# Moving the first state sums of units 0 and 1 behind one first-layer block in a fused RWKV-5 and SiLU kernel

## Chip, cores and metric

The kernel runs on one core of a Trainium2 chip. The metric is the device time of one execution in microseconds (us), given as the median over runs. The core has five engines with instruction queues of their own: TensorE (PE, with weight loads shown as PEld), VectorE (DVE), ScalarE (ACT), GpSimd (POOL) and SyncE (SP, which here only issues DMAs).

## What is computed

A recurrent attention (4 batches, 8 heads, 768 steps, head size 48), and behind it a two-layer network with SiLU on all 3072 tokens (width 384, hidden 2048):

```python
for t in range(S):
    kt, vt, rt = k[:, :, t], v[:, :, t], r[:, :, t]
    cur = einsum('bhd,bhe->bhde', u[None] * kt, vt)
    y[:, :, t] = einsum('bhd,bhde->bhe', rt, state + cur)
    state = w[None, :, :, None] * state + einsum('bhd,bhe->bhde', kt, vt)
...
x = y.transpose(0, 2, 1, 3).reshape(B * S, H * D)
h = x @ w_in
g = h * (1.0 / (1.0 + exp(-h)))
out = g @ w_out
```

## The kernel before

The sequence is cut into 6 chunks of 128 steps; a chunk of one batch is a **unit**, numbered chunk by chunk, so units 0 to 3 are the first chunk of the four batches, units 4 to 7 the second, and so on to 23. For a unit the kernel turns r and k on TensorE (step T), weights them with powers of the decay on VectorE (rT, kT), multiplies them to scores (P, or D for two units at once), masks these (n, m), and multiplies with v to get the outputs (V, Z). The term with u is formed on GpSimd (ku, ru, vu) with a sum on VectorE (rd). The state that a unit hands to the next chunk of its batch is a sum over its 128 steps of decayed k times v: kc is that decayed k (GpSimd, step kc), v16 the cast v (ScalarE, step v16). For units of the first chunk there is no state to add to, so the sums of a pair of batches come from one step, S (`first_sums`), into one PSUM buffer "sp". Two steps read it: st copies it to the running state `st` on VectorE, and scA (ScalarE) or sc (VectorE) copies it in f16 into the layout that the next chunk's outputs read.

The outputs of a chunk, turned (yT) and copied (xT on ScalarE, xTD on VectorE), feed the network. L*b.f* is a block of its first layer: the matmuls of hidden slices from f on for the batches that b names ("0" batches 0 and 1, "2" batches 2 and 3, both with two slices of 256 columns, so six matmuls; "4" all four batches, one slice of 512 columns, three matmuls). G*b.f* is its SiLU on ScalarE. The second layer follows later (line 628), spread as filler between the attention steps of later units.

All PSUM tiles of these steps except the turned inputs and the scores share one tag, "moe", with four buffers. A new tile takes the buffer that has been free longest, and its first write waits for the last reader of the tile before. The weights win (four pieces, i_q) and wout (four pieces, i_o) are loaded by GpSimd's queue, nearly all of r, k and v by SyncE's.

The order of instructions is the program's own (a manual schedule): no scheduler changes it. For the first eight units it is a string of steps, `order`, which a loop runs word by word; from unit 6 on a loop over pairs of units follows. Each engine runs its own instructions in the order of that string. The steps around the change are S0 (sums of units 0 and 1, line 419), L0.6 and G0.4 (lines 606 and 615), xT2 and xTD3 (line 595), kc1 and kc2 (line 248), st0 (line 441), scA0 (line 430), and further on Q4 (sums of units 4 and 5, line 478).

```python
def first_sums(i):
    sp = ps.tile([128, 512], FP, name="sp", tag="moe", bufs=4)
...
    for p in range(NP):
        for e in range(2):
            for j in range(2):
...
                    kc[(i + e) % NIN][:, h, :], L(i + e)["v16"][:, h, :],
```

So S0 goes through the four head pairs p, and in each takes unit 0 (two heads j), then unit 1.

Of the kernel before, what the change touches and what calls it, by code (L numbers as in the profile page):

```python
# [16 lines left out]
def kernel(  # L17
# [13 lines left out]
    B, H, S, D = r.shape  # L31
# [127 lines left out]
    lamC = cst.tile([128, H, D], FP)  # L159
    lamH = cst.tile([128, H, D], FP)  # L160
# [4 lines left out]
    lamN = cst.tile([128, H, D], FP)  # L165
# [522 lines left out]
    def piece(word, f):  # L688
# [30 lines left out]
        ur kz0 id itr lr0 wy pd0 ak0 cz2 kz3 itc wr mk wx cz1 mh lnw eK cg3 lamK kz4 kz1 lk1  # L719
        id16 lr1 pd3 lr3 lk3 clear 6*spin lv0 cg0 lv1 kz7 ak2 ar2 ku0 lv3 lv2 kz2 lr5 ub pd1 lv4  # L720
        lr4 lk4 lv5 pd2 lk5 lk7 lr6 lk6 uc T0 1*spin T1 lr7 lv7 kT0 pa4 rT0 ru0 ku1 v160 pd5 lv6
        rT1 kz6 rd0 kT1 wb ru1 P0 n0 2*spin rd1 P1 i_q0 vu0 lnwb T2 n1 v161 2*spin lamC lamH lamN pa6 pa7 V0 tab rT2 e0 kT2 ku2 T3 1*spin yT0 V1 kz5 i_q1 vu1 ru2 xT0 e1 P2 yT1 kT3 rT3
        rd2 ku3 xT1 v162 P3 ru3 n2 rd3 v163 n3 L0.0 vu2 kc0 1*spin G0.0 vu3 V2 L0.2 V3 G0.2 L0.4
        e2 i_q2 e3 kc1 yT2 yT3 S0 G0.4 xT2 xTD3 kc2 L0.6 L2.4 G0.6 st0 L2.0 scA0 v164 kc3 L2.6
        ku4 i_q3 v165 L2.2 T4 rT4 kT4 G2.4 ru4 G2.2 T5 G2.0 G2.6 L4.8 G4.8 L4.10 kT5 G4.10 L4.9
        kc4 ku5 S2 L4.11 rd4 rT5 st2 sc2 kc5 sd4 ru5 G4.9 G4.11 rA4 vu4 i_o0 Q4 D4 rA5 s1_4 ku7
        L4.12 rd5 vu5 m4 s2_4 G4.12 L4.13 G4.13 T6 Z4 L4.14 G4.14 L4.15 z4 yT4 2*spin yT5 i_o2
        i_o1 ku6 xT4 xT5 rT6 T7 G4.15 rT7 v167 sd6 kT6 v166 ru6 lr8 kc6 kc7 H H rd6 i_o3 H vu6
        lr9 rP7 rA6 sn4 H H lk8 lk9 sx4 lv9 lv8 ru7 kT7
    """  # L730
    for word in order.split():
        if "*" in word:
# [119 lines left out]
```

## Time and profile before

| | us |
|---|---|
| median of 3 runs | 184.46 |
| lowest and highest run | 183.74, 186.0 |
| profiled execution, its own time | 184.8 |
| span in its profile | 183.1 |

The span runs from the first to the last instruction of the profiled execution. Its granted TensorE clock is 1.0 throughout. Numbers with an L are lines of the kernel. In a timeline row stand the start, the length, the engine, line, operation, the tiles written and read, the shapes and the number of instructions merged; in brackets, the idle time of the engine before them and what ended it. In a row of a stretch stand its length, then for PE, PEld, DVE, ACT and POOL the busy time and the instructions, then the granted clock, the share of the 16 DMA engines and GB/s.

### The profile page before, as it was taken

Reading aid. Unit: us, or ns where it says so; the run is one execution under the profiler, and the core shown is the slowest. Engines: PE = TensorE matmul, PEld = TensorE weight load, DVE = VectorE, ACT = ScalarE, POOL = GpSimd, SP = SyncE. Lnnn points to the kernel's source line nnn. Section 1 sums busy time; section 2 is a strip of 40 time slices with the busy share of each in tenths; the row PEclk is TensorE's granted clock in tenths of the full one; section 3 lists DMA queues with packets and bytes.
Section 4 is the critical chain, followed back from the end, with each engine's and each line's share of the span. In section 5 each row is a group of like instructions: output and inputs, shape, how many; then the busy total and the mean of one; then the engine's idle time right before and its main releaser. Section 6 shows DMA issues by size and latency. Waiting matters only on the chain.

```text
span 183.1 us, 6612 instructions
## 1 busy us (share of the span) xinstructions
PE 175.7 (96%) x2801; PEld 114.1 (62%) x2801; DVE 116.1 (63%) x227; ACT 117.1 (64%) x212; POOL 129.3 (71%) x179
## 2 busy tenths in 40 slices
PE   7998899999999999999999899999999999999993
PEld 2566695588657976656547556647656566555562
DVE  4699729797798975955956945866944974000120
ACT  4468478599236796398687378787677781299100
POOL 7999999998899989959979769879769700000000
PEclk9999999999999999999999999999999999999999
DMA  5999999899588999999799999599699201410022
GB/s 90 238 218 196 196 195 196 138 216 222 99 174 211 159 213 197 178 188 206 130 183 150 181 194 185 127 183 184 156 200 245 48 4 47 129 43 0 12 77 86
DMA packets 102865, 27.89 MB, mean 152 GB/s; under 512 B 97586, under 2 KB 102324, under 8 KB 102836
## 3 DMA queue, kind: packets, MB, share of 16 engines
q1 hardware_dynamic: 97184, 23.67, 66.2%
q0 software_dynamic: 2176, 3.15, 10.1%
q10 hardware_dynamic: 3476, 0.66, 1.8%
q8 instruction: 22, 0.36, 0.8%
q14 instruction: 7, 0.06, 0.1%
HBM read 20.45 MB, written 4.72 MB: 137 GB/s over the span
## 4 chain that ended last, share of the span: by engine, by line
PE 76%; POOL 9%; DMA 5%; issue 3%; DVE 2%; ACT 2%; POOLq 0%; ACTq 0%; SPq 0%
PE ops L628 29%; PE hps L606 28%; PE att L455 5%; PE att L272 4%; DMA blocks<-planes 3%; POOL ku L240 2%; DMA kin<-in_k_dram 2%; PE sp L478 2%; PE zs L181 2%; POOL rku_f L245 2%; PE ops L653 1%; POOL vu L258 1%; PE yp L561 1%; PE yp L552 1%; ACT kT L326 1%
## 5 line engine op out<-in xcount | busy, mean ns | idle before, releaser
L606 PE MATMUL hps<-xT,win 128*128 128x512 f16 (+1 forms) x360 | 66.3, 338 | 0.0
L615 ACT ACTIVATE gT<-hps 128x512 f16<-128x512 f32 x96 | 55.3, 598 | 13.0 <-PE hps L606 9.8
L628 PE MATMUL ops<-wout,gT 128*128 128x384 f16 x368 | 63.0, 326 | 0.3
L606 PEld LDWEIGHTS <-win 128*128 128x128 f16 x360 | 38.8, 114 | 21.0 <-issue 0.2
L628 PEld LDWEIGHTS <-gT 128*128 128x128 f16 x368 | 35.0, 98 | 24.3 <-ACT gT L615 1.4
L401 DVE TENSOR_TENSOR y<-yp,vu 64x384 f16<-64x384 f32 (+1 forms) x34 | 18.9, 556 | 11.3 <-PE yp L561 6.1
L245 POOL TENSOR_TENSOR rku_f<-ku,u_bc 128x384 f32<-128x384 f32 x24 | 24.0, 1001 | 1.7 <-DVE u_bc L208 0.4
L240 POOL TENSOR_TENSOR ku<-kin,rin 128x384 f32<-128x384 f32 x24 | 24.5, 1020 | 0.0
L258 POOL TENSOR_TENSOR vu<-vin,rku 128x384 f32<-128x384 f32 x24 | 19.6, 829 | 6.4 <-DVE rku L253 6.3
L634 ACT COPY osb<-ops 128x384 f32<-128x384 f32 x20 | 9.4, 476 | 17.5 <-PE ops L628 11.8
L289 DVE TENSOR_TENSOR rT<-att,lamR 112x512 f16<-112x512 f32 (+1 forms) x26 | 17.8, 685 | 4.1 <-PE att L272 3.8
L326 ACT COPY kT<-blocks 112x1024 uint16<-112x1024 uint16 x14 | 15.6, 1161 | 7.3 <-DMA blocks<-planes 7.2
L495 DVE TENSOR_TENSOR s<-sp,sdec 112x384 f32<-112x384 f32 x10 | 5.6, 558 | 15.9 <-PE sp L478 15.3
L636 DVE COPY osb<-ops 128x384 f32<-128x384 f32 x3 | 1.7, 558 | 21.3 <-PE ops L628 21.3
L462 DVE TENSOR_TENSOR am<-att,maskH 128x1024 f16<-128x1024 f32 x10 | 12.2, 1224 | 3.7 <-PE att L455 3.7
L343 DVE TENSOR_TENSOR rX<-att,lamR 48x256 f16<-48x256 f32 x32 | 13.5, 422 | 0.5
L314 POOL TENSOR_TENSOR lnw_bc<-kin,lamN 128x384 f32<-128x384 f32 x7 | 7.0, 999 | 8.1 <-DMA kin<-in_k_dram 5.3
L253 DVE TENSOR_REDUCE rku<-rku_f 128x8 f32<-128x384 f32 x24 | 12.5, 545 | 0.3 <-POOL rku_f L245 0.3
L434 ACT CAST s1h<-s 48x384 f16<-48x384 f32 x16 | 8.2, 509 | 6.7 <-DVE s L495 6.6
L455 PE MATMUL att<-rT,kT 48*64 48x64 f32 x640 | 11.9, 220 | 0.5 <-issue 0.5
L455 PEld LDWEIGHTS att<-rT,kT 48*64 48x64 f32 x640 | 10.6, 135 | 0.6 <-issue 0.6
L263 ACT CAST v<-vin 128x384 f16<-128x384 f32 x16 | 7.8, 510 | 4.2 <-DMA vin<-in_v_dram 4.1
(106 smaller groups left out, 215.9 us busy)
## 6 DMA issues: line engine op xcount, KB each, us to landing
vin<-in_v_dram SPq DMA_DIRECT2D x24, 192.0 KB, 4.2
rin<-in_r_dram SPq DMA_DIRECT2D x23, 192.0 KB, 4.2
out_dram<-osb SPq DMA_DIRECT2D x23, 192.0 KB, 3.3
kin<-in_k_dram SPq DMA_DIRECT2D x22, 192.0 KB, 3.7
win<-in_moe_w_in_dram POOLq DMA_DIRECT2D x4, 384.0 KB, 6.8
wout<-in_moe_w_out_dram POOLq DMA_DIRECT2D x4, 384.0 KB, 6.6
kin<-in_k_dram ACTq DMA_DIRECT2D x2, 192.0 KB, 3.7
rin<-in_r_dram ACTq DMA_DIRECT2D x1, 192.0 KB
```

The lines of the kernel that those rows point to most:

```text
L240: eng.tensor_tensor(out=L(i)["ku"], in0=kin[i % NIN][:, :, 0:D], in1=rin[i % NIN][:, :, 0:D], op=ALU.mult)
L245: eng.tensor_tensor(out=L(i)["rku_f"], in0=L(i)["ku"], in1=u_bc, op=ALU.mult)
L253: nc.vector.tensor_reduce(out=L(i)["rku"], in_=L(i)["rku_f"], axis=mybir.AxisListType.X, op=ALU.add)
L258: eng.tensor_tensor(out=L(i)["vu"], in0=vin[i % NIN], in1=L(i)["rku"].unsqueeze(2).broadcast_to([128, H, D]), op=ALU.mult)
L289: nc.vector.tensor_tensor(out=L(i)[key].rearrange("p g (y t) -> p y g t", y=2), in0=L(i)["t"][0:PR, :, x], in1=lam, op=ALU.mult)
L326: nc.scalar.copy(out=L(i)["kT"].rearrange("p g t -> p (g t)").bitcast(U16) .rearrange("p (n y) -> p n y", y=2), in_=turned[0:PR, i % 2].re ...
L343: nc.vector.tensor_tensor(out=rx[here], in0=L(i)["t"][there, x, 0], in1=(lamM if by_planes(i) else lamR)[there, :, 0:HC], op=ALU.mult)
L401: nc.vector.tensor_tensor(out=y16[a], in0=y[b, 0:HD], in1=vu[a], op=ALU.add)
L455: nc.tensor.matmul(a[o0:o0 + HC, j, e, p, :], kT[r0:r0 + D, p, HC * x:HC * x + HC], rT[r0:r0 + D, p, HC * x:HC * x + HC], start=True, stop ...
L606: nc.tensor.matmul(hps[:, f, :].rearrange("p (b t) -> p b t", b=nb), win[(ft + f) // 4].rearrange("p q (t c) -> p q t c", c=4) [:, q, :, ( ...
L615: nc.scalar.activation(out=gts[sc][:, ft:ft + m, b0 * C:(b0 + nb) * C], in_=hpss[b0, ft], func=AF.Silu)
L628: nc.tensor.matmul(opss[b], gts[sc][:, ft, b * C:(b + 1) * C], wout[:, ft, :], start=(ft == 0), stop=(ft == NFT - 1))
```

## The change

S0 is moved in the string from behind yT3 to behind L0.6, ahead of L2.4. The lines below it are wrapped anew; no other word changes its place.

```diff
-        e2 i_q2 e3 kc1 yT2 yT3 S0 G0.4 xT2 xTD3 kc2 L0.6 L2.4 G0.6 st0 L2.0 scA0 v164 kc3 L2.6
+        L0.4 e2 i_q2 e3 kc1 yT2 yT3 G0.4 xT2 xTD3 kc2 L0.6 S0 L2.4 G0.6 st0 L2.0 scA0 v164 kc3
```

More of the change, by code (lines that the diff above doesn't have):

```diff
@@ L721 @@
         lr4 lk4 lv5 pd2 lk5 lk7 lr6 lk6 uc T0 1*spin T1 lr7 lv7 kT0 pa4 rT0 ru0 ku1 v160 pd5 lv6
-        rT1 kz6 rd0 kT1 wb ru1 P0 n0 2*spin rd1 P1 i_q0 vu0 lnwb T2 n1 v161 2*spin lamC lamH lamN pa6 pa7 V0 tab rT2 e0 kT2 ku2 T3 1*spin yT0 V1 kz5 i_q1 vu1 ru2 xT0 e1 P2 yT1 kT3 rT3
-        rd2 ku3 xT1 v162 P3 ru3 n2 rd3 v163 n3 L0.0 vu2 kc0 1*spin G0.0 vu3 V2 L0.2 V3 G0.2 L0.4
-        e2 i_q2 e3 kc1 yT2 yT3 S0 G0.4 xT2 xTD3 kc2 L0.6 L2.4 G0.6 st0 L2.0 scA0 v164 kc3 L2.6
[L725 to L729, printed above, removed]
+        rT1 kz6 rd0 kT1 wb ru1 P0 n0 2*spin rd1 P1 i_q0 vu0 lnwb T2 n1 v161 2*spin lamC lamH
+        lamN pa6 pa7 V0 tab rT2 e0 kT2 ku2 T3 1*spin yT0 V1 kz5 i_q1 vu1 ru2 xT0 e1 P2 yT1 kT3
+        rT3 rd2 ku3 xT1 v162 P3 ru3 n2 rd3 v163 n3 L0.0 vu2 kc0 1*spin G0.0 vu3 V2 L0.2 V3 G0.2
+        L0.4 e2 i_q2 e3 kc1 yT2 yT3 G0.4 xT2 xTD3 kc2 L0.6 S0 L2.4 G0.6 st0 L2.0 scA0 v164 kc3
+        L2.6 ku4 i_q3 v165 L2.2 T4 rT4 kT4 G2.4 ru4 G2.2 T5 G2.0 G2.6 L4.8 G4.8 L4.10 kT5 G4.10
+        L4.9 kc4 ku5 S2 L4.11 rd4 rT5 st2 sc2 kc5 sd4 ru5 G4.9 G4.11 rA4 vu4 i_o0 Q4 D4 rA5 s1_4
+        ku7 L4.12 rd5 vu5 m4 s2_4 G4.12 L4.13 G4.13 T6 Z4 L4.14 G4.14 L4.15 z4 yT4 2*spin yT5
+        i_o2 i_o1 ku6 xT4 xT5 rT6 T7 G4.15 rT7 v167 sd6 kT6 v166 ru6 lr8 kc6 kc7 H H rd6 i_o3 H
+        vu6 lr9 rP7 rA6 sn4 H H lk8 lk9 sx4 lv9 lv8 ru7 kT7
     """
```

## The prediction

> **What bounds the kernel now.** I read the page first (busy shares, slices), then the chain of waits in order of time, then the timeline around the moved step, then who waited for whom on TensorE. The page:
>
> ```profile
> PE 175.7 (96%) x2801; PEld 114.1 (62%) x2801; DVE 116.1 (63%) x227; ACT 117.1 (64%) x212; POOL 129.3 (71%) x179
> ...
> PE   7998899999999999999999899999999999999993
> ...
> POOL 7999999998899989959979769879769700000000
> ...
> DMA  5999999899588999999799999599699201410022
> ...
> DMA packets 102865, 27.89 MB, mean 152 GB/s; under 512 B 97586, under 2 KB 102324, under 8 KB 102836
> ```
>
> TensorE (PE) is the only engine that is full (9 is 90% or more) in every slice from the ninth to the last but one; GpSimd (POOL) and the DMA engines are full only in the first two thirds. A busy PE need not be a PE at its rate, so I look at how fast it goes, in the chain of waits in order of time (start, length, what), and at stretches of the span:
>
> ```profile
> 21.57 1.01 POOL kc L248
> ...
> 22.64 0.40 PE sp L419 x14
> 23.04 3.40 PE hps L606 x30
> ...
> 48.48 7.26 PE ops L628 x44
> ```
>
> ```profile
> 21.50:33.00 11.50, 10.55 (x212) 8.05 (x211) 6.58 (x14) 9.40 (x19) 11.46 (x14) 1.00 1.05 181
> 33.00:70.00 37.00, 37.00 (x711) 28.17 (x713) 30.59 (x59) 24.24 (x44) 34.42 (x44) 1.00 0.94 182
> ```
>
> 44 second-layer matmuls of 384 columns take 7.26 us, 165 ns each, or 2.3 columns a ns; 30 first-layer matmuls of 256 columns take 3.40 us, 113 ns each, the same rate. From 33 to 70 us PE is busy for all of 37.00 us at a granted clock of 1.00. What can still be won there is nothing; between 21.5 and 33 us PE is idle for 0.95 us (11.50 less 10.55), and there GpSimd is busy for 11.46 of 11.50 us. The moved step lies in that stretch.
>
> **The change.** S0 is 16 small matmuls with their weight loads (line 419, kc of units 0 and 1 against v16) into one PSUM buffer. It issues nothing on any other engine and no DMA. It moves behind G0.4, xT2 (ScalarE), xTD3 (VectorE), kc2 (GpSimd) and L0.6 (PE); as the engines have orders of their own, the only order that changes is PE's: S0 and the six matmuls of block L0.6 change places. PE before:
>
> ```profile
> 21.52 0.50 PE L591 MATMUL yT<-ident,y 128*128 128x128 f16 x6
> 21.94 0.21 PE L419 MATMUL sp<-v,kc 128*64 128x48 f16 x2
> 22.64 0.40 PE L419 MATMUL sp<-v,kc 128*64 128x48 f16 x14 [0.48 <-POOL kc L248]
> 22.97 3.47 PE L606 MATMUL hps<-xT,win 128*128 128x256 f16 x30
> 26.37 0.43 PE L272 MATMUL att<-ident,rin 64*112 64x64 f32 x8
> ...
> 27.41 2.13 PE L606 MATMUL hps<-xT,win 128*128 128x512 f16 x9
> ...
> 30.61 0.44 PE L478 MATMUL sp<-v,kc 64*64 64x48 f16 x32
> ...
> 32.48 0.33 PE L455 MATMUL att<-rT,kT 48*64 48x64 f32 x3 [0.47 <-issue]
> 32.75 1.49 PE L606 MATMUL hps<-xT,win 128*128 128x512 f16 x6
> ```
>
> The first two matmuls of S0 (unit 0) start at 21.94, the third (unit 1) waits for kc1, which GpSimd ends at 21.57 + 1.01 = 22.58, and starts at 22.64; the queue behind it holds L0.6 and all further PE work. This is the stall that goes. The other engines around it:
>
> ```profile
> 20.35 1.18 DVE L401 TENSOR_TENSOR y<-yp,vu 128x384 f16<-128x384 f32 x2
> ...
> 20.75 0.80 POOL L84 DMA_DIRECT2D win<-in_moe_w_in_dram x1
> ...
> 21.57 2.92 POOL L248 TENSOR_TENSOR kc<-kin,lamC 128x384 f16<-128x384 f32 x3
> 21.71 0.60 ACT L615 ACTIVATE gT<-hps 128x512 f16<-128x512 f32 x1 [0.82 <-PE hps L606]
> ...
> 22.05 0.36 DVE L595 COPY xT<-yT 128x384 f16<-128x384 f16 x1 [0.52 <-PE yT L591]
> ...
> 22.21 0.47 ACT L595 COPY xT<-yT 128x384 f16<-128x384 f16 x1
> ...
> 23.09 0.56 DVE L441 COPY st<-sp 112x384 f32<-112x384 f32 x1 [0.68 <-PE sp L419]
> ...
> 23.85 0.60 ACT L615 ACTIVATE gT<-hps 128x512 f16<-128x512 f32 x1 [1.17 <-PE hps L606]
> 24.35 0.94 ACT L430 CAST blocks<-sp 48x384 f16<-48x384 f32 x2
> ...
> 25.41 0.80 POOL L84 DMA_DIRECT2D win<-in_moe_w_in_dram x1
> ...
> 29.12 0.99 POOL L248 TENSOR_TENSOR kc<-kin,lamH 128x384 f16<-128x384 f32 x1
> ...
> 38.82 1.97 POOL L248 TENSOR_TENSOR kc<-kin,lamH 128x384 f16<-128x384 f32 x2
> ```
>
> *L0.6 first.* It may start when S0 did, at 21.94: its inputs were there for L0.4, and the PSUM buffer that it now takes (S0's) is free when VectorE has read unit 3's output, at 20.35 + 1.18 = 21.53. Six matmuls of 113 ns: until 21.94 + 0.68 = 22.62.
>
> *S0 behind it.* It takes the buffer that L0.6 had, which G0.4 leaves at 21.71 + 0.60 = 22.31, before 22.62: the wait that the swap adds costs nothing. kc1 is done at 22.58 and was seen by PE 0.06 us later, at 22.64: at most 0.02 us of waiting is left. 14 matmuls took 22.97 - 22.64 = 0.33 us, so 16 take 0.38: until 23.00.
>
> *L2.4 then.* Its buffer and input come from the copies that end at 22.68 (ScalarE) and 22.41 (VectorE), so it starts at 23.00. Before it came six matmuls after 22.97, at 23.65. Gain on PE: 0.65 us.
>
> *Consumers of S0.* The copy to st was at 23.09, as S0's last matmul was issued just before 22.97; now that is 23.00, so 0.03 us later, with VectorE idle until PE's turns of unit 4. The silu of L0.6 (23.85) needs only L0.6 and ScalarE free at 22.68, so it comes near 22.8, and the two casts of the state (24.35) follow it near 23.4, or near 23.7 if they stay behind the copy to st as in the trace. Either way ScalarE's whole row moves 0.6 to 0.9 us ahead, and the block L2.2 that reuses S0's buffer, now near 24.97, comes after their end (24.4 to 24.6). Cost nothing; if that cover were gone it would be PE waiting out at most the 0.94 us of the casts.
>
> *What is late next.* GpSimd does not move: it was full. So I walk PE's later joins with it and with the loads.
>
> ```profile
> DMA to landing us min/median/max: 5.6/5.6/5.6
> ```
>
> ```profile
> DMA to landing us min/median/max: 6.7/6.7/6.7
> ```
>
> These two rows are the third and fourth piece of win, from the view of that tile cut to each issue. Piece 2 lands at 20.75 + 5.6 = 26.35; L4.8 wants it at 27.41 - 0.65 = 26.76: no wait. Q4 (sp of units 4 and 5, 30.61) wants kc5, done at 29.12 + 0.99 = 30.11 and seen near 30.17; it would now start at 29.96, do its four matmuls of unit 4 and wait until 30.17. So from here on the gain is no longer 0.65 but about 30.61 - 30.17 = 0.44, plus hardly 0.05 for the four that are done: I take 0.45. Piece 3 lands at 25.41 + 6.7 = 32.11; L4.12 wants it at 32.75 - 0.45 = 32.30: 0.2 us to spare. Q6 wants kc7, done at 38.82 + 1.97 = 40.79; the PE timeline puts it at
>
> ```profile
> 41.81 0.38 PE L478 MATMUL sp<-v,kc 64*64 64x48 f16 x24
> ```
>
> and 41.81 - 0.45 = 41.36 is later than 40.79. The 0.47 us without a releaser at 32.48 stands in the middle of a group; I leave it as it is (bounds: 0 to 0.9 us, that is gone or doubled; the middle, since the instructions ahead of it are the same in number).
>
> *Sum.* 0.45 us off 184.8 us, the profiled execution's own time (span 183.1 and 1.7 around it): 184.35. The median of the three runs shown is 184.46, 0.34 below that execution, so 184.46 - 0.45 = 184.0 us. Bounds of the gain: 0.65 if GpSimd's kc5 comes a little sooner, 0 if a later wall takes all.
>
> **The rivals.**
>
> *GpSimd or the loads are the pace, and the gain is absorbed.* For it: GpSimd busy 11.46 of 11.50 us, DMA share 0.94 to 1.05 until 70 us, and 0.2 us of the gain already lost at kc5. If a later product or landing in the first two thirds was just in time, the rest is lost there: 184.46, no change. Against it: after 33 us PE waits for nobody, and the joins that I could price have 0.2 to 0.6 us to spare. [...]
>
> *Slower: the transposes of the k planes land later.* PE's earlier start shifts later loads against each other. The place is where the trace has no slack:
>
> ```profile
> 84.96 6.35 DMA blocks<-planes
> ...
> 91.39 0.93 ACT kT L326
> ...
> 93.61 1.48 ACT gT L615 x3
> ```
>
> ```profile
> DMA to landing us min/median/max: 4.4/5.4/6.3
> ```
>
> ScalarE stands in kT behind that transpose, the silus stand behind kT, and PE's second layer (95.14) behind the silus. A landing there later by d costs PE d. It decides from d = 0.45 on. The seven transposes spread from 4.4 to 6.3 us, so a d of 1.9 is the measured spread: 184.46 - 0.45 + 1.9 = 185.9. For it: DMA share 0.99 between 70 and 102 us. Against it: this one was already the slowest of the seven. To be 2% slower (3.7 us) takes 4.1 us, more than two such spreads, at several turns of the loop, or a stall of a kind that the trace does not show.
>
> *It does not do what it says*: S0 or L0.6 waits for the other's buffer and the stall moves. The ends 21.53 and 22.31 leave 0.4 and 0.3 us, so I give it little: 184.5, no change.
>
> **How the numbers follow.** Forecast (gain 0.2 to 0.65): 0.59. Absorbed: 0.18. No effect through the buffers: 0.03. Slower: 0.17, of which 0.10 beyond 2%, as several turns or an unseen stall. Faster by more than 2%: 0.03; all idle time of PE between 21.5 and 33 us is 0.95 us, far less than 3.7, so this is only measurement. The three runs of before spread from 183.74 to 186.0, so about 2% is what a measurement of this kernel can tell from no change. Within 2%: 0.59 + 0.18 + 0.03 + 0.07 = 0.87. The range takes the forecast's own ends (183.8 to 184.3), the scatter of the median downwards (0.72, the lowest run) to 183.1, and upwards the absorbed case with its scatter and most of one late transpose, to 185.5.
>
> **What would show it.** Right: the row of S0 has 16 matmuls in one piece with no wait for kc, L0.6 starts near 21.94, L2.4 near 23.0, and Q4 shows a short wait for kc of about 0.2 us near 30. The silu of L0.6 comes near 22.8 and the casts near 23.5. From there each PE row lies 0.45 us earlier to the end. Wrong: a PE wait for ScalarE or VectorE ahead of L0.6 or S0; PE rows that are back at their old times at 42 or 70 us (absorbed, and the row in front names the wall); a longer landing of a plane transpose with a PE wait for gT behind it (slower).

## The result

| | us |
|---|---|
| before, median of 22 runs | 184.49 (183.48 to 186.0) |
| changed, median of 22 runs | 183.50 (182.51 to 185.77) |
| ratio of the two | 0.9945, 95% interval 0.9924 to 0.9966 |
| profiled execution of the changed kernel, its own time and span | 184.6, 182.9 |

The kernel is faster by 0.55%, about 1.0 us (by the interval 0.6 to 1.4). The profiled execution of the changed kernel is 1.1 us above its median, so its page does not show where the median's gain is from. On TensorE's timeline (start, length, then what, with the idle time before it in brackets) it shows a wait that the profile of before lacked:

```profile
18.40 0.85 PE L606 MATMUL hps<-xT,win 128*128 128x256 f16 x6 [0.57 <-DMA win<-in_moe_w_in_dram]
...
21.40 0.85 PE L606 MATMUL hps<-xT,win 128*128 128x256 f16 x6 [0.87 <-DMA win<-in_moe_w_in_dram]
22.08 0.50 PE L591 MATMUL yT<-ident,y 128*128 128x128 f16 x6
22.41 0.82 PE L606 MATMUL hps<-xT,win 128*128 128x256 f16 x6
23.16 0.43 PE L419 MATMUL sp<-v,kc 128*64 128x48 f16 x16
23.53 2.81 PE L606 MATMUL hps<-xT,win 128*128 128x256 f16 x24
...
30.51 0.44 PE L478 MATMUL sp<-v,kc 64*64 64x48 f16 x32
30.78 1.13 PE L455 MATMUL att<-rT,kT 48*64 48x64 f32 x61
32.70 0.33 PE L455 MATMUL att<-rT,kT 48*64 48x64 f32 x3 [0.79 <-issue]
```

The second row is block L0.4. It stood at 20.83 before and now starts 0.57 us later, because the second piece of win landed late; the fourth is L0.6, the fifth S0, in one piece and with no wait. With L0.4 that late, kc1, which GpSimd ended near 22.2, would have been ready for S0 in the old order too. Still L2.4 (23.53) starts 0.12 us earlier than before (23.65): the order is as planned, and the execution was an unlucky one. Its rows at 42 and 70 us stand 0.1 to 0.2 us later than before. The last row is a gap that was 0.47 us before and is 0.79 us here, with no releaser.

A second profile of the same kernel, taken with the experiments, is a more usual execution (span 181.6 us):

```profile
20.30 0.84 PE L606 MATMUL hps<-xT,win 128*128 128x256 f16 x6
20.98 0.50 PE L591 MATMUL yT<-ident,y 128*128 128x128 f16 x6
21.31 0.82 PE L606 MATMUL hps<-xT,win 128*128 128x256 f16 x6
22.06 0.59 PE L419 MATMUL sp<-v,kc 128*64 128x48 f16 x16
22.58 2.81 PE L606 MATMUL hps<-xT,win 128*128 128x256 f16 x24
...
26.41 0.44 PE L272 MATMUL att<-ident,kin 64*112 64x64 f32 x8 [0.20 <-DMA kin<-in_k_dram]
...
29.97 0.44 PE L478 MATMUL sp<-v,kc 64*64 64x48 f16 x32
30.25 1.15 PE L455 MATMUL att<-rT,kT 48*64 48x64 f32 x64
31.33 1.49 PE L606 MATMUL hps<-xT,win 128*128 128x512 f16 x6
```

From L0.4 to L2.4 it takes 22.58 - 20.30 = 2.28 us, against 23.65 - 20.83 = 2.82 before: 0.54 us gained by the order. And D4 (line 455) now stands as 64 matmuls in one piece: the gap without a releaser is gone. From the start of D4 to the block behind it are now 31.33 - 30.25 = 1.08 us, against 32.75 - 30.88 = 1.87 before. So the gap cost 0.79 us and not only the 0.47 us of idle time in its row, which counts from the end that the profile gives to the matmul ahead (30.88 + 1.13 = 32.01).

This pair of profiles does not measure the change by itself. From L0.4 to Q4 (line 478) only 0.11 us of the 0.54 are left (9.67 us against 30.61 - 20.83 = 9.78), because the turn for k of unit 5, the row at 26.41, waits for its load. Of the 1.5 us between the two spans, 0.53 us lie ahead of L0.4, where no word was changed, and 0.55 us at a second gap like that in D4, near 100 us: 0.71 us in the profile of before, 0.16 us here. The profiles of the old order with the stall doubled and with the loads held (below) lack that second gap too, so its absence is not the change's doing. The experiments are about the stall of S0 and the gap in D4.

### The profile page after: what moved, and what is told of

It is laid out like the page before. It is cut to its first block, busy times and chain, and to the rows that moved or that the text cites. A ratio compares the mean times of both kernels' runs of the same rounds, so it can differ in the third digit from the quotient of the medians.

```text
span 182.9 us, 6612 instructions
## 1 busy us (share of the span) xinstructions
PE 174.6 (96%) x2801; PEld 113.8 (62%) x2801; DVE 116.1 (63%) x227; ACT 117.4 (64%) x212; POOL 129.4 (71%) x179
## 4 chain that ended last, share of the span: by engine, by line
PE 74%; DMA 10%; POOL 7%; issue 3%; DVE 2%; ACT 2%; SPq 0%; POOLq 0%; ACTq 0%
PE ops L628 29%; PE hps L606 29%; PE att L455 5%; DMA win<-in_moe_w_in_dram 4%; PE att L272 4%; DMA blocks<-planes 4%; DMA kin<-in_k_dram 2%; PE sp L478 2%; POOL ku L240 1%; PE ops L653 1%; PE yp L561 1%; PE yp L552 1%; POOL rku_f L245 1%; ACT gT L615 1%; POOL planes L317 1%
## 5 line engine op out<-in xcount | busy, mean ns | idle before, releaser
L289 DVE TENSOR_TENSOR rT<-att,lamR 112x512 f16<-112x512 f32 (+1 forms) x26 | 17.8, 684 | 3.5 <-PE att L272 3.1
```

Source lines behind the costliest of these rows:

```text
L289: nc.vector.tensor_tensor(out=L(i)[key].rearrange("p g (y t) -> p y g t", y=2), in0=L(i)["t"][0:PR, :, x], in1=lam, op=ALU.mult)
```

## The experiments

Each kernel was timed against the kernel before on the same chip; the intervals are 95%. The first runs compare the stall of S0 with causes elsewhere.

**The changed kernel again** (no edit).

> The changed kernel once more, for a second profile and time. Stall theory (TensorE's wait for kc1 in front of S0 is all that the change removes): S0 shows no wait for kc, L2.4 starts 0.65 us earlier than with the old order against the same start of L0.4, and the ratio to before lies between 0.995 and 0.998. Rival (the gain is larger than that stall because the order also moves ScalarE's casts and silus ahead, which frees something later): the ratio is 0.994 or lower and the profile shows TensorE still gaining on before after 27 us.

Ratio 0.9956 (0.993 to 0.9982). The first theory's range is met at its lower edge, and the profile above, which is of this run, shows more than it allowed: 0.54 us from the stall and D4 without its gap.

**The stall doubled, in the old order.**

```diff
-        e2 i_q2 e3 kc1 yT2 yT3 S0 G0.4 xT2 xTD3 kc2 L0.6
+        e2 i_q2 e3 kc2 kc1 yT2 yT3 S0 G0.4 xT2 xTD3 L0.6
```

> The old order with kc1 behind kc2 on GpSimd: S0's wait doubles by one operation of 0.97 us. Stall theory: TensorE is behind nothing else there, so the whole 0.97 us reaches the end, ratio 1.005. Absorption rival (a later wait for GpSimd or a load sets the pace anyway): the rows of TensorE are back at their times of before by Q4 or Q6, ratio under 1.002.

Ratio 1.0041 (1.0011 to 1.0071), 0.75 us. TensorE's timeline:

```profile
23.22 0.40 PE L419 MATMUL sp<-v,kc 128*64 128x48 f16 x14 [1.28 <-POOL kc L248]
...
33.73 0.33 PE L455 MATMUL att<-rT,kT 48*64 48x64 f32 x3 [1.14 <-issue]
```

S0 waits 1.28 us instead of 0.48, and all of this 0.8 us reaches Q4: from L0.4 to Q4 it takes 31.20 - 20.61 = 10.59 us, against 9.78 before. So nothing is absorbed up to there; the ratio's interval (0.2 to 1.3 us) leaves open whether a part is later. The gap in D4 is longer too in this profile, 1.14 us against 0.47.

**S0 two blocks later.**

```diff
-        L0.6 S0 L2.4 G0.6 st0 L2.0 scA0
+        L0.6 L2.4 S0 G0.6 st0 L2.0 scA0
```

> The changed order with S0 one block later still, behind L2.4. Stall theory: the stall is gone already after one block, so the second brings 0 to 0.1 us; ratio to before the same as that of the changed kernel within 0.002. Rival (later is better for ScalarE's or the buffers' sake): a further gain of 0.3 us or more, ratio 0.002 or more below the changed kernel's. L2.4 may wait up to 0.1 us for the copy of unit 2.

Ratio 1.0002 (0.9976 to 1.0027): the gain is gone, which neither theory expected. TensorE, and then ScalarE, in its timeline:

```profile
21.50 1.70 PE L606 MATMUL hps<-xT,win 128*128 128x256 f16 x12
23.13 0.43 PE L419 MATMUL sp<-v,kc 128*64 128x48 f16 x16
23.50 1.50 PE L606 MATMUL hps<-xT,win 128*128 128x256 f16 x12
25.27 0.82 PE L606 MATMUL hps<-xT,win 128*128 128x256 f16 x6 [0.28 <-ACT blocks L430]
...
32.04 0.33 PE L455 MATMUL att<-rT,kT 48*64 48x64 f32 x3 [0.38 <-issue]
```

```profile
21.86 0.47 ACT L595 COPY xT<-yT 128x384 f16<-128x384 f16 x1
22.36 0.60 ACT L615 ACTIVATE gT<-hps 128x512 f16<-128x512 f32 x1
24.26 0.96 ACT L430 CAST blocks<-sp 48x384 f16<-48x384 f32 x2 [1.31 <-DVE st L441]
```

The casts of the state stay behind the copy to st, end at 25.22, and the block L2.2 that reuses S0's buffer waits for them, 0.28 us. The prediction had put this cover at some 0.4 us for one block; in the second profile of the changed kernel it was about 0.25 us (the casts end at 24.31, L2.2 starts near 24.57), and one block more uses it up. L0.6 and L2.4, the first row, take 0.2 us longer than the twelve matmuls behind S0: L2.4 waits for ScalarE's copy of unit 2, which ends at 21.86 + 0.47 = 22.33. The gap in D4 is there as well.

**The stall taken away by other means: kc1 on VectorE.**

```diff
+    def stand_in(i):
+        nc.gpsimd.tensor_tensor(out=spare[:, :, 0:D], in0=kin[i % NIN][:, :, 0:D], in1=lamC, op=ALU.mult)
...
-        e2 i_q2 e3 kc1 yT2 yT3 S0
+        e2 i_q2 e3 kd1 du1 yT2 yT3 S0
```

Here kd1 is the same product on VectorE, and du1 the stand-in.

> S0 stays where it was; kc1 is made by VectorE ahead of the turned copies, so that S0 need not wait, and GpSimd does an operation of the same size into a spare tile in kc1's place, so that its pace stays. Stall theory: S0's wait falls from about 0.5 us to under 0.1 us and the time falls as with the change, ratio 0.995 to 0.998. Rival (the order itself brings the gain, by ScalarE's rows moving ahead): the wait goes, but the time stays, ratio 0.998 to 1.002.

Ratio 1.0244 (1.0212 to 1.0277), slower where both theories had the same or faster. It does not decide between them, since the wait did not go but grew to 3.95 us (timeline of the three engines, then two stretches):

```profile
21.06 4.53 DVE L248 TENSOR_TENSOR kc<-kin,lamC 128x384 f16<-128x384 f32 x1
...
21.31 1.01 POOL L254 TENSOR_TENSOR spare<-kin,lamC 128x384 f16<-128x384 f32 x1
22.27 1.94 POOL L248 TENSOR_TENSOR kc<-kin,lamC 128x384 f16<-128x384 f32 x2
24.18 0.98 POOL L240 TENSOR_TENSOR ku<-kin,rin 128x384 f32<-128x384 f32 x1
25.11 0.80 POOL L84 DMA_DIRECT2D win<-in_moe_w_in_dram  x1
...
25.64 0.58 PE L424 MATMUL sp<-v,kc 128*64 128x48 f16 x14 [3.95 <-DVE kc L248]
```

```profile
26.00:30.50 4.50, 4.50 (x31) 3.19 (x27) 0.56 (x1) 2.78 (x6) 4.50 (x5) 0.53 1.09 185
31.00:35.00 4.00, 4.00 (x64) 2.58 (x62) 2.80 (x5) 3.05 (x6) 0.93 (x2) 1.00 1.01 200
```

What this shows of the hardware is told at the end.

The next runs take away the stall alone, and try the gap in D4. Its cause may lie in the DMA packets. The page of before counts 22 packets in queue q8, which is marked "instruction", 0.36 MB, so 16 KB each; TensorE has 5,627 instructions in the trace, which makes 256 to a packet (an estimate from these two counts, if all 22 packets are TensorE's). Ahead of the gap stand 961 of TensorE's instructions in the trace, and ahead of a second one (0.71 us at 101.25) 3,521: ten times 256 more. So the theory is that TensorE has run out of instructions there and waits for the next packet.

**The stall alone, in the old order.** This kernel takes kc of unit 0 for unit 1 too, so its state of unit 1 is wrong; it leaves out only the wait.

```diff
-                        kc[(i + e) % NIN][:, h, :], L(i + e)["v16"][:, h, :],
+                        kc[(i + e if i else 0) % NIN][:, h, :], L(i + e)["v16"][:, h, :],
```

> The old order, but S0 uses kc of unit 0 for unit 1 too, so that it does not wait for kc1 (the first state of unit 1 is then not the reference's); every instruction is there as before. Stall theory: S0's wait is gone, TensorE is 0.65 us ahead from L0.6 on, and the ratio to before equals that of the change, 0.994 to 0.997. Rival (the gain of the change comes from the new order of ScalarE's work or from the buffers): ratio 0.998 or more.

Ratio 0.9973 (0.9943 to 1.0003): it does not tell the two apart by itself. The profile (span 180.9 us) does:

```profile
21.39 0.43 PE L419 MATMUL sp<-v,kc 128*64 128x48 f16 x16
...
29.41 0.77 PE L478 MATMUL sp<-v,kc 64*64 64x48 f16 x32
30.02 1.15 PE L455 MATMUL att<-rT,kT 48*64 48x64 f32 x64
```

S0 has no wait; Q4 (second row) now takes 0.77 us instead of 0.44, which is the wait for kc5 that the prediction named, 0.33 us; and D4 is in one piece. From L0.4 (20.27) to the block behind D4 (31.10) it takes 10.83 us, against 32.75 - 20.83 = 11.92 before, with ScalarE's order and the buffers as they were.

**The loads held back.** In the old order, SyncE's loads of r and v of unit 7 and v of unit 6 wait for a one-column memset of rin behind kT4.

```diff
-        uc T0 1*spin T1 lr7 lv7 kT0 pa4 rT0 ru0 ku1 v160 pd5 lv6
+        uc T0 1*spin T1 kT0 pa4 rT0 ru0 ku1 v160 pd5
...
-        T4 rT4 kT4 G2.4
+        T4 rT4 kT4 ho7 lr7 lv7 lv6 G2.4
```

> The old order; the loads of r and v of units 7 and of v of unit 6 are held back on SyncE by a one-column memset behind kT4, so that they are issued near 28.4 us and not from 26.3 us on. Fetch theory (the idle 0.47 us in the middle of D4 is TensorE waiting for its next 16 KB of instructions, whose DMA stands behind those loads): that packet starts within 1.5 us of the first instruction of its forerunner, the gap in D4 goes, S0's wait stays; ratio 0.997 to 0.999. Rival (the gap is something else): the gap stays at 0.4 us or more; ratio 1.000 or more.

Ratio 1.0016 (0.9992 to 1.004), and the gap stays:

```profile
32.13 0.33 PE L455 MATMUL att<-rT,kT 48*64 48x64 f32 x3 [0.51 <-issue]
```

In this profile the load of r of unit 7 is issued at 28.02 us and the two of v from 28.43 us on, and the packet still starts only at 29.66 us, 3.0 us after the piece of instructions ahead of it began (table below). So it is not these loads that the packet waits for. The load queue as a whole is not excluded: other loads filled the time, and its share from 26 to 29 us was 45.3%, against 46.6% before. **The same in the changed order:**

> The changed order with the same loads held back. Fetch theory: no gap in D4 in any profile, ratio to before 0.9935 to 0.996, that is the stall of S0 (0.65 us) and the gap (0.47 us) together, and not much under that of the changed kernel, which mostly loses the gap already because it asks for the instructions earlier. Rival (the two have nothing to do with each other): the held loads make no difference or cost, ratio 0.996 or more.

Ratio 0.9959 (0.993 to 0.9988), as the changed kernel without it; in the profile the gap is 1.05 us, where the theory had none. That execution also ran for a while at half the granted clock:

```profile
18.50:20.50 2.00, 2.00 (x17) 1.32 (x16) 1.78 (x3) 0.60 (x1) 2.00 (x4) 0.50 1.23 218
```

**The ends of the packets moved,** in the old order, by more and smaller instructions at the start.

```diff
-        id16 lr1 pd3 lr3 lk3 clear 6*spin lv0
+        id16 lr1 pd3 lr3 lk3 clear 2*spin tiny lv0
```

> The old order; four of the six matmuls that only warm TensorE at the start give way to 32 tiny ones, so that every later instruction stands 56 places further back and the ends of the 16 KB pieces of instructions fall 56 instructions earlier in the program. Fetch theory: the gap leaves D4, and with it its place in the turns near 101 us; gaps, if any, stand 56 instructions earlier (193 less 56 modulo 256). Ratio 0.997 to 1.002, as new ends may fall on other dense groups. Rival (the gap belongs to D4 itself): it stays at the same matmul of D4.

In the profile of before, the six matmuls at the start, from 2.97 us on, come 0.43 us apart, and the two of the same shape at 10.44 us come 0.22 us apart; that the first bring on the faster pace is the author's reading, which no run tests.

TensorE in its timeline (the lines are 5 higher here, so 460 is D4 and 566 is 561 of before):

```profile
30.79 1.15 PE L460 MATMUL att<-rT,kT 48*64 48x64 f32 x64
...
100.68 0.36 PE L566 MATMUL yp<-v,am 64*64 64x48 f16 x21 [0.86 <-issue]
```

D4 has no gap, and the gap near 100 us has left the turns for the outputs ahead of them, while it still has 3,521 instructions ahead of it. The gap belongs to the packet and not to the instruction. The ratio, 1.0044 (1.001 to 1.0079), is above what was expected. The profile has a wait of 0.7 us for a load of k near 48 us, where the others have 0.2 us at most; the runs scatter from 183.6 to 189.6 us, and what made them slower is not shown.

With the further profiles, the packet can be put beside TensorE's own time. The first column is the start of TensorE's instruction number 705, with which the piece of 256 begins that ends at D4's gap; the second the start of the instruction packet; the third says how many of the 400 packets of the fourth piece of win, which begin at 26.6 to 26.9 us in all these rows, start behind it; then the gap by its idle time, and the time from D4's start to that of the block behind it.

| kernel | no. 705 | packet | win 4 behind it | gap in D4 | D4 to next block |
|---|---|---|---|---|---|
| S0 without the wait | 25.90 | 26.31 | 400 | none | 1.08 |
| changed, second profile | 26.41 | 27.42 | 371 | none | 1.08 |
| loads held | 26.70 | 29.66 | 14 | 0.51 | 1.89 |
| two blocks | 26.74 | 29.72 | 0 | 0.38 | 1.76 |
| changed, loads held | 26.96 | 30.42 | 0 | 1.05 | 2.44 |
| changed, first profile | 26.99 | 30.45 | 2 | 0.79 | 2.18 |
| before | 27.09 | 30.08 | 36 | 0.47 | 1.87 |
| stall doubled | 27.68 | 31.45 | 0 | 1.14 | 2.53 |

Up to 26.41 the packet comes within about 1.0 us, ahead of nearly all of that piece; from 26.70 on it comes 3.0 to 3.8 us later, when the piece is all but through. Number 705 is a yardstick and not what asks for the packet: later in the trace of before, packets start up to 2.7 us ahead of the instruction in that place. The block behind D4 pays 0.3 us more than the idle time says in every row with a gap. And the gap ends with the packet: in all profiles of this case together, ten gaps of 0.3 us or more stand at ends of packets, and each ends 1.3 to 1.6 us after its packet has been carried.

What the DMA queues did is in their packets, MB and share of the 16 engines' time: before from 26 to 29 us, with no packet in q8; before from 29 to 32 us; then the changed kernel's second profile from 26 to 29 us (q0 is GpSimd's queue, which carries win here, q1 that of the loads of r, k and v).

```profile
q0 software_dynamic: 206, 0.21, 60.2%
q1 hardware_dynamic: 1403, 0.26, 46.6%
```

```profile
q1 hardware_dynamic: 2463, 0.47, 83.7%
q0 software_dynamic: 195, 0.18, 36.5%
q8 instruction: 1, 0.02, 1.9%
```

```profile
q0 software_dynamic: 313, 0.32, 70.4%
q1 hardware_dynamic: 1666, 0.31, 51.9%
q8 instruction: 1, 0.02, 2.2%
```

The last runs test that: the fourth piece of win is issued one operation earlier.

**In the old order:**

```diff
-        ku4 i_q3 v165 L2.2
+        i_q3 ku4 v165 L2.2
```

> The old order of TensorE; GpSimd issues the fourth piece of win one operation (1.0 us) earlier, ahead of ku4. Theory of the queue (in D4 TensorE waits for instructions whose 16 KB packet is served only when the packets of that piece are through; they ran from about 27.0 to 30.2 us before): the piece runs from about 26 to 29 us, the instruction packet starts near 29 and not 30, and the gap in D4 falls from about 0.5 us to 0 to 0.1; S0's wait stays; ratio 0.997 to 0.998. Rival (the packet is late for another reason, the loads of r, k and v or the fetch itself): the gap stays at 0.4 us or more, ratio 0.999 or more.

Ratio 0.9975 (0.995 to 0.9999), as the theory of the queue has it. In the profile the packet starts at 29.29, with number 705 at 27.12 and 2 of the piece's packets behind it, and D4 has no gap:

```profile
22.26 0.40 PE L419 MATMUL sp<-v,kc 128*64 128x48 f16 x14 [0.69 <-POOL kc L248]
...
27.12 0.44 PE L272 MATMUL att<-ident,kin 64*112 64x64 f32 x8 [0.24 <-DMA kin<-in_k_dram]
...
30.96 1.15 PE L455 MATMUL att<-rT,kT 48*64 48x64 f32 x64
```

Its price is in the second row: a load of k, for the turn of unit 5, now comes late. With it and a longer wait of S0, L0.4 (20.19) to the block behind D4 (32.04) takes 11.85 us, against 11.92; so the profile shows the gap gone, but not where the ratio's gain is from. **The same in the changed order:**

> The changed order with the same earlier issue. Theory of the queue: no gap in D4 in the profile, S0 without a wait; ratio to before 0.9935 to 0.995, at or a little under that of the changed kernel. Rival: as the changed kernel, with a gap in D4 in some executions, ratio 0.9945 to 0.996.

Ratio 0.9972 (0.9945 to 1.0), above the range of the theory: no gap in D4, but a wait of 0.65 us for that load of k, so nothing is won over the changed kernel. **With the second piece earlier too** (i_q1 ahead of ku2):

> As the one before, and the second piece of win is issued one operation (1.0 us) earlier too, ahead of ku2. If block L0.4 waits for that piece in many executions (it landed at 21.35 us in the profile of the changed kernel, 0.87 us late, and at 20.25 us in the second one, in time), it now lands near 19.5 to 20.3 and the wait goes: ratio 0.002 under that of the one before it. If the wait is rare, no difference (within 0.001).

Ratio 0.9986 (0.9957 to 1.0015), where 0.002 less was expected if L0.4 often waits, and the same if not. L0.4 no longer waits, and D4 has no gap, yet the price has grown to a wait larger than both:

```profile
27.88 0.44 PE L272 MATMUL att<-ident,kin 64*112 64x64 f32 x8 [1.65 <-DMA kin<-in_k_dram]
```

**With kc5 ahead of ku5,** beside the fourth piece:

> As the second, with kc5 and ku5 in each other's place on GpSimd, so that kc5 is there 1.0 us earlier. The prediction held that Q4 waits for kc5 and loses 0.2 of the 0.65 us: if so, TensorE is 0.15 to 0.2 us further ahead from Q4 on, ratio 0.001 lower than without the swap. If S0's gain is held up elsewhere, no difference.

Ratio 0.9959 (0.9937 to 0.9981). The difference to the kernel without the swap (0.9972) is inside the intervals, and in the profile TensorE comes to Q4 only at 30.56, when both orders have kc5: not settled. None of these came out faster than the changed kernel.

## Why the prediction came out right, and what it missed

- *The stall of S0.* Right. It is gone in both profiles, L0.6 fills it, and the swapped buffers cost nothing. The size holds where kc1 is late: 0.54 us between L0.4 and L2.4 in the second profile, where 0.65 was forecast; S0's third matmul still waits about 0.13 us there, against at most 0.02 in the forecast. Where L0.4 itself is late for want of win, it is near nothing.
- *Consumers.* Right for one block; the cover was 0.25 us and not some 0.4, because the casts stay behind the copy to st, and the run with two blocks uses it up.
- *Q4 waiting for kc5.* Right as a mechanism: 0.33 us where TensorE is far enough ahead (S0 without the wait). In the two profiles of the changed kernel it is not there, as TensorE was not that early.
- *The loads.* Incomplete: the pieces of win were priced for L4.8 and L4.12, but the second piece (L0.4, 0.87 us late in one execution) and the load of k for unit 5 were not. The latter is 0.20 us of idle time in the second profile, yet with it the 0.54 us have shrunk to 0.11 us at Q4.
- *The 0.47 us in D4.* This is the step that was mis-sized. It was taken as unchanged, with bounds of 0 to 0.9 us, and priced by its idle time; by the starts around it, it cost 0.79 us. In the runs it stands at the end of a piece of 256 instructions and ends 1.3 to 1.6 us after the next packet has been carried, so it is read here as TensorE's wait for instructions, and its length goes with when that packet comes: 0, 0.79 and 1.05 us of idle time in three profiles of the changed order (the last with the loads held), 1.14 us with the stall doubled. With the whole gap gone the sum is 0.45 + 0.79 = 1.24 us, a ratio of 0.993, which lies in the interval of the result; 0.45 alone, 0.9976, lies outside it. The measured 0.9945 is between the two, as it would be if the gap goes in a part of the executions.
- *The total.* The gain was forecast as 0.45 us and measured as 1.0 us (0.6 to 1.4). That the time still fell into the range of 183.1 to 185.5 is owed to the 0.7 us set aside there for scatter, and not to the sum. The sign that every later row lies 0.45 us earlier was seen in neither profile.
- *Absorption by GpSimd or the loads.* Not for this change as a whole (0.9945), though the load of k took some 0.4 us in the second profile; in the profiles of the further edits it is again the load of k that takes what D4 gains.
- *Late transposes.* No profile shows TensorE waiting more than 0.2 us for a silu behind the transposes of the k planes. Another transposing DMA, that of the outputs (xT), held TensorE for 0.32 us at 77.95 in the second profile of the changed kernel.

Shown is that the wait of S0 goes, that the gap sits at the end of a piece of 256 instructions and ends 1.3 to 1.6 us after the next packet has been carried, that it goes when TensorE is at number 705 by 26.41 us, and that it goes when the fourth piece of win is issued earlier. That the packet stands in a line behind that piece is the reading that fits all of the rows above, not a thing that a row names; with the second piece earlier too, the packet came while 105 packets of the piece were still to start. Not shown is how the 1.0 us is shared out between the stall and the gap. In what share of executions the changed kernel escapes the gap stays open: one of its two profiles does, and the one that does not is 1.1 us above the median.

## What to carry to other kernels

A short wait at the head of an in-order queue was worth filling with independent work that was ready, but look how long the cover lasts: one block was right here (ratio 0.9945), two put a buffer's release on the path, with a wait of 0.28 us for it, and gave all back (1.0002). An "issue" gap in the middle of a group of equal instructions cost 0.79 us here, where its idle time said 0.47: price such a gap by the starts around it, count the instructions between two of them (2,560 here, ten times 256), and look what else uses the DMA engines when the instruction packet is due. The DMA share here was 1.05 from 21.5 to 33 us, and with a piece of win issued earlier TensorE's wait for a load of k came to 0.24 us in the old order, where the profile of before has none, and to 0.65 and 1.65 us in the changed one, where the profiles of the changed kernel have 0.20 us at most; so price the load that is pushed back as well.

## What the runs showed of the hardware that was not expected

- TensorE's instructions came in packets of 16 KB (22 in queue q8 of before), whose time the profile counts on the same 16 DMA engines as that of the data (0.8% of the span, beside 66.2% for the loads' queue q1). In the rows of the table such a packet started 0.4 to 3.8 us after the forerunner's first instruction; these 256 instructions were used up in some 5 us (27.09 to 32.0 before), and TensorE stood still for up to 1.14 us.
- A VectorE product of two operands in SBUF took 4.53 us beside a GpSimd that ran one operation after another, and ended only after GpSimd went over to issuing a DMA at 25.11; VectorE's bonus addition of the same size, with one operand in PSUM, took 0.56 us right ahead of it. Four operations of GpSimd ran in a row during the product, from 21.31 to 25.16, though by its row the product had started first. In the profile of before, another VectorE product in SBUF alone (line 306, 112x384) took 0.56 us at 45.45, with no GpSimd operation beside it, and 1.26 us at 59.31, beside two of them. That GpSimd holds such a product up is a reading that fits these times; no run separates the two engines to prove it.
- In the run with kc1 on VectorE the mean granted clock was 1.00 from 15 to 20 us, 0.73 from 21.5 to 25.6, 0.53 from 26 to 30.5 and 1.00 from 31 to 35. If it fell once to 0.50 and rose once, it was 0.50 from about 23.4 to 30.2 us, an estimate from these means. 19 first-layer matmuls took 4.22 us there (from 26.15), 0.22 us each, where 30 took 3.47 us in the profile of before, 0.12 us each. TensorE's idle stretch began near 21.7 us, so by that estimate the clock fell some 1.7 us into it; from 21.5 to 25.6 us TensorE was busy for 0.19 us. In the changed order with the loads held, the mean was 0.64 from 17.5 to 18.5 us, 0.50 to 20.5 and 0.83 to 22.5, so by the same estimate 0.50 from 17.8 to 21.2 us; between 14 and 17.8 us TensorE had stood still for 0.46 and for 0.85 us. Five other profiles with a wait of 0.9 us at the place of the second have a mean clock of 0.998 to 1.0 over the whole span, so the runs give no rule for it.
